# Six rows of a head per partition for q, k and v, with natural order restored on the way out of PSUM

## The chip, the core and the metric

One core of a Trainium2 chip runs the whole kernel. The metric is device time in microseconds (us), the median of several executions. The engines are PE (matrix products and transposes), ACT, DVE and POOL (elementwise work) and SP. SP issues the loads of q, k and v. POOL issues the loads of the weights, which are cast from fp32 to bf16 on the way, and can also compute.

## The reference

```python
# attention with a forget gate: B=8, H=8, S=576, D=64
scores = q @ k^T / sqrt(D);  cum = cumsum(log(clip(f)))
attn = softmax(where(causal, -1e9, scores + cum_i - cum_j))
x = (attn @ v) as (B, S, 512)
# spectral mixing: 64 complex modes, each with its own 512x512 weights (real and imaginary)
X = rfft(x, axis=1);  Y[:, :64] = X[:, :64] * (w_r + i w_i)   # per mode
u = x + irfft(Y);  out = u + relu(u @ w_ch)
```

The weights w_r and w_i are 134 MB of fp32; q, k and v are 28 MB together. Nothing is read twice.

## The kernel before

The attention has 32 steps. A step is one batch element `b` and one pair of heads, and `dc` numbers the pairs. Steps 0 to 7 are all batch elements of the first pair. The mode products of a pair need all eight batch elements, so they start after step 8 is under way. From then on each step also does two of the 64 weight groups. A ring of nine buffers prefetches weight groups.

```python
def emit_loads(s):                       # on SP, three stage tiles per tensor
    for d, src in zip(QKVst[s % STG], (q, k, v)):
        for h in range(2):
            nc.sync.dma_start(           # two rows of a head per partition: runs of 512 B
                d[:, h, 0:4, :].rearrange("p (a r) d -> p a (r d)", r=2),
                src[b, 2 * dc + h, 0:512, :].rearrange("(a p r) d -> p a (r d)", p=128, r=2))
        nc.sync.dma_start(d[0:64, :, 4, :], ...)   # the last 64 rows: runs of 256 B
...
for n in range(NRING):                   # on POOL, before anything else of substance
    emit_w_load(n)                       # two DMAs each, of 512 KB in bf16
nc.gpsimd.dma_start(wch[:], ...)
...
def emit_transposes(s):
    nc.scalar.copy(kb, stk_)             # ACT casts k
    nc.vector.tensor_copy(qb, stq_)      # DVE casts q
    nc.vector.tensor_tensor(va, stv_, decay, mult)   # DVE scales v: ready for attn @ v
    # k and q: five PE transposes each; contiguous evacuations, k on ACT, q on DVE
...
for s in range(NS + 1):
    emit_loads(s + 2); emit_transposes(s + 1)
    # scores, exp (ACT), causal masks (DVE), attn @ v, DFT of step s - 1
    if s > B:                            # modes: two weight groups a step
        for j in range(2):
            emit_modes(2 * (s - B - 1) + j)
            next_w()                     # POOL issues the next weight group
```

Because a partition holds rows 2p and 2p+1, the rows are in an interleaved order in this kernel, and its masks and its score blocks are arranged for that.

The softmax here doesn't subtract the row's maximum and nothing guards it: scores larger than these inputs give would overflow.

## Time and profile before

The median was 534.56 us (533.92 to 534.80, 3 runs). The profiled execution has a span of 533.4 us.

| stretch of the span, us | what happens | what limits it |
|---|---|---|
| 0 to 72 | weight prefetch, first steps | loads of q, k, v, about 12 us each |
| 72 to 118 | steps 3 to 9 | ACT, 5.66 us a step |
| 127 to 395 | steps and modes | loads again, DMA always full |
| 395 to 477 | rest of the weights | weight DMA |
| 477 to 533 | output | PE, ACT and DVE |

The first lines are from the page's table of 40 slices: the busy share in tenths for ACT and the DMA engines, and what the DMA moved in GB/s. Destination bytes are counted, so a weight byte of bf16 stands for two bytes read.

```profile
ACT  1033299997407152534264442554472332226564
...
DMA  9999985559999999999999999999999999982554
GB/s 160 212 212 213 211 199 153 146 148 209 212 212 212 211 212 212 211 211 212 212 212 213 212 211 213 212 212 211 209 207 207 206 207 207 207 136 90 218 226 178
```

The next view has the busy time of each engine in the stretches of the table above. Its last three columns are the granted PE clock, the DMA share, and GB/s. The share can exceed 1 because the records of packets overlap: with weights alone it is as high (1.21 from 395 to 477 us), since a weight packet is recorded at about 97 ns and one comes about every 80 ns on an engine.

```profile
core 0: us, PE busy (x) PEld busy (x) DVE busy (x) ACT busy (x) POOL busy (x), PEclk, DMA share, GB/s
0.00:72.00 72.00, 13.64 (x110) 9.29 (x112) 20.59 (x69) 19.44 (x24) 15.73 (x29) 0.91 1.16 203
72.00:118.00 46.00, 34.71 (x546) 25.75 (x553) 41.86 (x116) 45.52 (x66) 0.10 (x1) 1.00 0.57 155
127.00:395.00 268.00, 133.53 (x2552) 113.62 (x2570) 112.85 (x315) 116.02 (x158) 57.96 (x78) 0.69 1.21 211
395.00:477.00 82.00, 63.26 (x969) 41.83 (x979) 38.38 (x64) 23.62 (x40) 19.26 (x26) 0.95 1.21 202
477.00:533.00 56.00, 50.65 (x276) 23.87 (x279) 32.53 (x51) 30.22 (x53) 0.00 (x0) 0.96 0.45 171
```

In the second stretch ACT is busy 45.5 of 46 us while the DMA is half idle. In the third no engine is busy half the time, and the DMA is full. The chain of waits (start, duration, what) says which transfers matter:

```profile
11.51 12.14 DMA stq_115<-in_q_dram
...
48.50 11.97 DMA stv_114<-in_v_dram
...
87.66 1.56 ACT E_125 L385 x2
...
176.30 12.40 DMA stk_119<-in_k_dram
...
414.77 20.28 DMA wb<-in_moe_w_r_dram
```

The loads carry 28 MB against 134 MB of weights, yet they are the chain. The reason is in the queue table, here for 200 to 240 us (packets, MB, share of the 16 engines); q0 has the weights, q1 the loads:

```profile
q0 software_dynamic: 5916, 5.88, 86.4%
q1 hardware_dynamic: 5914, 2.54, 34.0%
```

The packets pair off one for one. A load packet has 512 or 256 B, and each one waits for a weight packet of 2048 B read. Last, two lines of POOL's timeline: the last initial issue, and the first issue after the modes have freed a ring buffer. I call the latter the first reissue; before it the ring is full.

```profile
45.11 0.74 POOL L214 DMA_DIRECT2D wch<-in_moe_w_ch_dram  x1 [2.74 <-DMA wb<-in_moe_w_r_dram]
117.90 0.74 POOL L80 DMA_DIRECT2D wb<-in_moe_w_r_dram  x1 [72.05 <-PE A L99]
```

### The profile page before, as it was taken

To read this page: it belongs to the slowest core of one execution; us is meant where nothing else is said; L and a number is where in the kernel's file an instruction comes from. 1 tells how busy PE (TensorE), PEld (TensorE's weight loads), DVE (VectorE), ACT (ScalarE), POOL (GpSimd) and SP (SyncE) were. 2 spreads that over 40 slices of the span, in tenths; PEclk is the share of its full clock that TensorE was granted. 3 is DMA by queue.
4 is the path that set the end of the run, shared out by engine and by line. 5 is a ranking of instruction groups with operands and counts; after the bars stand their busy time and mean duration, and the time that the engine had idled before them with its cause. 6 is when DMAs were issued, how large, how long until landed. Compare 5 with 4: busy or idle time off the path is not lost.

```text
span 533.4 us, 11332 instructions
## 1 busy us (share of the span) xinstructions
PE 304.2 (57%) x4637; PEld 221.4 (42%) x4684; DVE 254.6 (48%) x636; ACT 243.8 (46%) x352; POOL 97.4 (18%) x139
## 2 busy tenths in 40 slices
PE   0013077687516254645266353565488886669996
PEld 0002055465415243534155242454476544444442
DVE  4132079996415344443046243453584544435765
ACT  1033299997407152534264442554472332226564
POOL 6221000014211221221222122122232222100000
PEclk9999689999756767676567765677797999989999
DMA  9999985559999999999999999999999999982554
GB/s 160 212 212 213 211 199 153 146 148 209 212 212 212 211 212 212 211 211 212 212 212 213 212 211 213 212 212 211 209 207 207 206 207 207 207 136 90 218 226 178
DMA packets 137236, 106.28 MB, mean 199 GB/s; under 512 B 19360, under 2 KB 134560, under 8 KB 137184
## 3 DMA queue, kind: packets, MB, share of 16 engines
q0 software_dynamic: 68112, 67.64, 75.4%
q1 hardware_dynamic: 69072, 37.92, 30.7%
q8 instruction: 36, 0.59, 0.4%
q14 instruction: 16, 0.13, 0.1%
HBM read 163.73 MB, written 9.44 MB: 325 GB/s over the span
## 4 chain that ended last, share of the span: by engine, by line
DMA 75%; PE 12%; ACT 7%; DVE 2%; issue 2%; SPq 1%; ACTq 0%; DVEq 0%; POOLq 0%
DMA wb<-in_moe_w_r_dram 15%; DMA stv_114<-in_v_dram 9%; DMA stq_115<-in_q_dram 9%; DMA stk_119<-in_k_dram 9%; DMA stk_116<-in_k_dram 7%; DMA stq_112<-in_q_dram 7%; DMA stv_120<-in_v_dram 5%; DMA stq_118<-in_q_dram 5%; DMA stv_117<-in_v_dram 5%; DMA stk_113<-in_k_dram 4%; ACT E_126 L385 2%; ACT E_125 L385 2%; PE pz L569 2%; PE pu L561 2%; PE pz L565 2%
## 5 line engine op out<-in xcount | busy, mean ns | idle before, releaser
L80 POOL DMA_DIRECT2D wb<-in_moe_w_r_dram x64 | 47.7, 745 | 320.8 <-PE A L99 231.8
L99 PEld LDWEIGHTS <-wb 128*128 128x128 bf16 x2048 | 63.7, 99 | 33.6 <-DMA wb<-in_moe_w_i_dram 12.3
L385 ACT ACTIVATE E_125<-ps 128x1024 bf16<-128x1024 f32 x64 | 58.4, 966 | 13.5 <-PE ps L378 13.2
L385 ACT ACTIVATE E_126<-ps 128x1024 bf16<-128x1024 f32 x64 | 58.5, 960 | 7.6 <-PE ps L378 6.2
L80 POOL DMA_DIRECT2D wb<-in_moe_w_i_dram x64 | 48.0, 751 | 37.4 <-DMA wb<-in_moe_w_i_dram 37.3
L513 ACT CAST XW<-pxw 128x512 bf16<-128x512 f32 x40 | 23.1, 586 | 57.7 <-PE pxw L506 56.5
L350 PE MATMUL tp<-ident_bf,qb 128*128 128x128 bf16 x160 | 18.5, 257 | 52.9 <-ACT XT_1330 L445 21.5
L434 PE MATMUL px<-bas,x_all 128*128 128x128 bf16 x160 | 22.6, 244 | 37.8 <-DVE x_all L419 37.1
L506 PE MATMUL pxw<-wch,xT 128*128 128x512 bf16 x148 | 38.8, 387 | 1.3 <-DVE xT L502 0.6
L378 PE MATMUL ps<-QTs,KTz_0_123 128*128 128x64 bf16 (+5 forms) x128 | 29.1, 304 | 17.6 <-ACT E_126 L385 15.0
L378 PE MATMUL ps<-QTs,KTz_0_121 128*128 128x64 bf16 (+5 forms) x128 | 27.2, 287 | 20.4 <-ACT E_125 L385 17.4
L410 PE MATMUL pav<-va,E_125 128*128 128x65 bf16 x544 | 31.1, 216 | 13.4 <-DVE E_125 L397 11.0
L330 ACT CAST kb<-stk_116 128x640 bf16<-128x640 f32 x11 | 8.0, 728 | 66.5 <-DMA stk_116<-in_k_dram 66.5
L113 DVE TENSOR_TENSOR YT<-A,Yacc 128x256 bf16<-128x256 f32 x16 | 20.8, 1298 | 35.8 <-PE A L99 35.8
L357 DVE COPY QTs<-tp 128x576 bf16<-128x576 bf16 x32 | 14.6, 456 | 42.1 <-PE tp L350 41.3
L350 PEld LDWEIGHTS <-qb 128*128 128x128 bf16 x160 | 13.6, 113 | 49.2 <-issue 49.1
L350 PE MATMUL tp<-ident_bf,kb 128*128 128x128 bf16 x160 | 17.4, 248 | 28.6 <-ACT kb L330 16.5
L410 PEld LDWEIGHTS <-E_125 128*128 128x128 bf16 x544 | 27.0, 114 | 16.0 <-DVE E_125 L397 11.6
L576 DVE SCALAR_TENSOR_TENSOR uo<-pz,uo 128x512 f32<-128x512 f32 (+1 forms) x40 | 26.8, 688 | 12.6 <-ACT uo L575 12.4
L419 DVE TENSOR_TENSOR x_all<-pav,rcp 128x384 bf16<-128x384 f32 x64 | 31.1, 487 | 0.9
L397 DVE TENSOR_TENSOR E_125<-E_125,mask_74 128x512 bf16<-128x512 bf16 (+1 forms) x80 | 28.8, 380 | 5.4 <-ACT E_125 L385 4.6
L397 DVE TENSOR_TENSOR E_126<-E_126,mask_74 128x512 bf16<-128x512 bf16 (+1 forms) x80 | 28.7, 380 | 5.5 <-ACT E_126 L385 4.9
(121 smaller groups left out, 619.6 us busy)
## 6 DMA issues: line engine op xcount, KB each, us to landing
wb<-in_moe_w_r_dram POOLq DMA_DIRECT2D x64, 512.0 KB, 20.3
wb<-in_moe_w_i_dram POOLq DMA_DIRECT2D x64, 512.0 KB, 21.4
out_dram<-uo SPq DMA_DIRECT2D x16, 512.0 KB, 2.6
stq_112<-in_q_dram SPq DMA_DIRECT2D x22, 128.0 KB, 12.0
stk_113<-in_k_dram SPq DMA_DIRECT2D x22, 128.0 KB, 11.9
stv_114<-in_v_dram SPq DMA_DIRECT2D x22, 128.0 KB, 11.9
stq_115<-in_q_dram SPq DMA_DIRECT2D x22, 128.0 KB, 12.4
stk_116<-in_k_dram SPq DMA_DIRECT2D x22, 128.0 KB, 12.1
```

The source lines that it names most:

```text
L80: nc.gpsimd.dma_start(wb[:, t, :, :], src[g * MG : (g + 1) * MG, dc * 128 : (dc + 1) * 128, :].rearrange("m p e -> p m e"),)
L99: nc.tensor.matmul(A[:, eb, mi, :], lhsT=wb[:, t, mi, eb * 128 : (eb + 1) * 128], rhs=XT3[:, m, c0 : c0 + 2 * B], start=(t == 0), stop=(t ...
L350: nc.tensor.transpose(tp[:, sc * 128 : (sc + 1) * 128], src[:, sc, :, :].rearrange("p h d -> p (h d)"), ident_bf[:, :],)
L378: nc.tensor.matmul(ps[:, h, o : o + n], lhsT=KTz[s % NK][h][:, jb * 128 : (jb + 1) * 128], rhs=QT[s][:, CB[jb] + c0 : CB[jb] + c0 + n], st ...
L385: nc.scalar.activation(E[:, :, piece * 512 : piece * 512 + w], ps[:, :, 0:w], ACT.Exp, scale=scale,)
L397: nc.vector.tensor_tensor(dg, dg, tr, ALU.mult)
L410: nc.tensor.matmul(pav[:, i, h, :], lhsT=E[:, h, c : c + 128], rhs=va[:, jb, h, :], start=(jb == 0), stop=(jb == top),)
L419: nc.vector.tensor_tensor(x_all[:, b, sbs[0] : sbs[0] + n, dc * 128 : (dc + 1) * 128].rearrange("p c (h d) -> p c h d", h=2), pav[:, 0:n, ...
L434: nc.tensor.matmul(px[:, :, :], lhsT=x_all[:, b, sb, dc * 128 : (dc + 1) * 128], rhs=bas[:, sb, :, :], start=(sb == 0), stop=(sb == NSB - 1),)
L506: nc.tensor.matmul(pxw[:, :], lhsT=xT[:, eb, sb * 128 : (sb + 1) * 128], rhs=wch[:, eb, :], start=(eb == 0), stop=(eb == NDC - 1),)
L513: nc.scalar.copy(XW[:, b, sb, :], pxw[:, :])
L576: nc.vector.scalar_tensor_tensor(o_sb[:Ms, :], pz[:Ms, :], 0.0, u_sb[:Ms, :], ALU.max, ALU.add)
```

## The change

The intent is longer runs in HBM: with six rows of a head per partition (96 partitions) a run has 1536 B and a step's three tensors need three DMAs. The transposes then come out in the order (row within partition, partition). The PSUM evacuation reads them with a stride and so puts q and k in natural order, which lets the masks and the score blocks shrink. v needs rows on partitions, so it is transposed, put in order, and transposed back. For the first eight steps the cast of k and the scaling of v move to POOL.

```diff
     def emit_loads(s):
-        for h in range(2):
-            nc.sync.dma_start(d[:, h, 0:4, :]..., src[...]"(a p r) d -> p a (r d)", p=128, r=2)
-        nc.sync.dma_start(d[0:64, :, 4, :], src[..., 512:576, :]...)
+        nc.sync.dma_start(d[:, :, :, :]..., src[b, 2*dc : 2*dc+2]."h (p r) d -> p h (r d)", r=6)
...
     def emit_transposes(s):
+        early = s < B
-        nc.scalar.copy(kb..., stk_)
+        nc.gpsimd.tensor_copy(kv, stk_) if early else nc.scalar.copy(kv, stk_)
-        nc.vector.tensor_tensor(va[..., 0:Dh], stv_..., decay, ALU.mult)
+        (nc.gpsimd if early else nc.vector).tensor_tensor(vb, stv_..., decay6, ALU.mult)
-        for which, src in (("k", kb), ("q", qb)):      # 5 transposes of 128 rows
+        for which, src in (("k", kb), ("q", qb), ("v", vb)):   # 6 transposes of 96 rows
...
-            nc.vector.tensor_copy(QTs[:, :], tp[:, 0:S])
+            tv = tp.rearrange("c r p -> c p r")
+            nc.vector.tensor_copy(QTs.rearrange("c (p r) -> c p r", r=6), tv)   # k, v: same on ACT
+    def emit_vback(s):                   # after the last scores of step s
+        # five transposes of VT, then DVE copies to va
...
-    EOFF = [0, 576, 1152, 1472, 1792]; EW = 1920
+    EOFF = [0, 576, 1024, 1344, 1536]; EW = 1664
-    tr = mask3 (256 columns);  top = min(sb | 1, 4)
+    tr = trimask (128 columns); top = sb
...
-    out[...].rearrange("(p r) e -> p r e", r=2)       # 4-KB runs
+    out[...].rearrange("(r p) e -> p r e", r=2)       # 2-KB runs
```

## The prediction

> **What bounds it now.** The span of 533.4 us has four stages.
> (a) 0 to 72 us: the chain of waits is q/k/v loads of about 12 us each, since the weight prefetch runs beside them.
> (b) 72 to 118 us: the weight ring is full, and modes cannot start before step 8 is done. The ACT timeline repeats every 5.66 us a step, ACT 99% busy; DMA is half busy.
> (c) About 127 to 395 us: DMA always full (share 1.21, 212 GB/s by destination bytes); the chain is again loads of 12 to 13 us.
> (d) 395 to 477 us: weights alone, at 206 GB/s of destination, twice that of source; then a 56-us tail on PE, ACT and DVE.
>
> In one 40-us window of (c), the queue table has 5916 weight packets and 5914 load packets: the engines take one of each in turn. This agrees with the Trainium skill, "DMA: Bandwidth & Descriptors", section on queues, rings and completion order (engines alternate between queues by packet). From the packet records, source traffic is 359 GB/s in (c), 411 in (d). A weight packet costs an engine about 80 ns (estimate, 2048 B x 16 / 411 GB/s), so a load packet of 512 or 256 B takes about 32 ns of the rest. A step has 120 load packets an engine, which wait for 120 weight packets: 13.4 us, while its two weight groups need 129.
>
> **What the change does.**
> - Loads: 36 packets of 1536 B an engine and step. At my estimate of 60 to 65 ns each (extrapolated from 18 ns for 256 B and 27 ns for 512 B when alone), a step costs the DMA 2.3 us in place of 3.7. Loads stop being the chain; in (c) the weights become it, DMA still full. About 20 steps' loads come after the modes start: 28 to 30 us saved, all on the critical path.
> - Start: for the first eight steps the cast of k and the scaling of v move to POOL, behind the 19 initial weight issues, the last of which left at 45.1 us because eight DMAs may be outstanding. With loads quickly out of the way it should leave near 39 us. So step 0 starts LATER than before (scores near 46 us), but no loads hold the next steps.
> - Compute a step: ACT loses the k cast (0.74 us, early steps) and 256 of 1856 score columns a head (0.5), gains a v evacuation (0.7): 5.4 us early, 6.1 later. DVE loses mask columns (0.6), gains a strided, larger v-back copy. PE gains 13 transposes and loses four of 34 AV products: under ACT. POOL about 3 us a step. First modes at 46 + 7x5.4 + 2x6.1 + 4.6 = 101 us, against 118: 17 us saved. In (c) the extra compute has slack (6 us of PE in 12 us, at a granted clock of 0.67).
> - Tail: same bytes, 2-KB runs out for 4-KB ones; DMA is half idle there: nothing.
>
> **Sum.** 534.6 - 17 - 29 = about 488 us. Range 475 to 504. Faster by over 2%: 0.97, within 2%: 0.025, slower: 0.005.
>
> **What would show it.** First POOL cast near 40 us; first weight reissue near 101 us; load packets of 1536 B at 60 to 75 ns; chain in (c) on weight DMAs, not loads; source rate there near 395 GB/s; weights done near 430 us; tail still 56 us.
>
> **What would make it wrong.** POOL's cast and scaling over 5.5 us a step, or held back by DVE; strided PSUM reads costing ACT or DVE over 1.5 times; the two-buffer transpose pool, now five tiles a step, stalling PE; 1536-B packets costing as much per byte as the short ones.

## The result, and the profile after

The changed kernel takes 497.18 us (496.21 to 498.16, 4 runs) against 534.68 us before in the same rounds. The ratio is 0.9296, with a 95% interval of 0.9268 to 0.9324. Ratios here are the mean time of one kernel's fast runs over that of the other's fast runs of the same rounds, so not quite the ratio of the medians. The result is correct. Timed again later beside the last experiment, it took 495.70 us (ratio 0.9282).

The same lines of the page's 40 slices, after:

```profile
ACT  2202788999883444444444446662003122236564
...
DMA  9999998449999999999999999999999999923655
GB/s 205 264 206 211 267 273 228 143 148 236 260 255 233 234 234 234 234 234 234 234 235 232 234 219 207 207 206 208 205 207 207 206 206 207 207 48 136 230 207 192
```

The engines' busy times by stretch, after:

```profile
core 0: us, PE busy (x) PEld busy (x) DVE busy (x) ACT busy (x) POOL busy (x), PEclk, DMA share, GB/s
0.00:44.00 44.00, 4.18 (x18) 2.62 (x18) 12.31 (x43) 6.38 (x8) 15.16 (x28) 1.00 1.13 222
44.00:86.00 42.00, 30.66 (x405) 22.94 (x406) 34.58 (x73) 32.90 (x50) 18.51 (x17) 0.92 1.10 254
86.00:110.00 24.00, 18.60 (x315) 14.03 (x314) 20.97 (x57) 23.39 (x37) 0.31 (x1) 1.00 0.45 136
118.00:275.00 157.00, 102.81 (x1911) 84.71 (x1911) 84.81 (x226) 85.04 (x128) 35.95 (x48) 0.76 1.20 239
285.00:440.00 155.00, 108.63 (x1677) 74.52 (x1675) 67.09 (x144) 53.46 (x85) 38.75 (x53) 0.79 1.21 203
440.00:496.00 56.00, 51.14 (x280) 24.12 (x276) 32.25 (x51) 30.12 (x53) 0.00 (x0) 0.96 0.46 169
```

The mixed stage moves 239 GB/s in place of 211. The stretch of the tail is 56 us as before. For 44 us at the start PE and ACT do almost nothing, although loads of the first steps have landed. POOL's timeline has the reason:

```profile
43.50 0.74 POOL L214 DMA_DIRECT2D wch<-in_moe_w_ch_dram  x1 [1.80 <-DMA wb<-in_moe_w_r_dram]
44.24 0.83 POOL L347 CAST kb<-stk_114 96x768 bf16<-96x768 f32 x1
45.04 1.48 POOL L355 TENSOR_TENSOR vb<-stv_115,wdec_79 96x768 bf16<-96x768 f32 x1
...
49.45 1.47 POOL L355 TENSOR_TENSOR vb<-stv_121,wdec_79 96x768 bf16<-96x768 f32 x1
...
109.69 0.82 POOL L82 DMA_DIRECT2D wb<-in_moe_w_r_dram  x1 [32.23 <-PE A L101]
```

ACT's exp of a step's first scores shows when the step starts; I call it the first scores. Step 0 is at 49.70 us and step 7 at 93.95 us:

```profile
49.70 1.02 ACT L426 ACTIVATE E_128<-ps 128x1024 bf16<-128x1024 f32 x1
...
93.95 1.02 ACT L426 ACTIVATE E_129<-ps 128x1024 bf16<-128x1024 f32 x1
```

The first cast of k stands behind 19 weight issues in POOL's program. The trace never shows more than eight weight DMAs between issue and landing, so the later issues wait for earlier weights to land, and the cast waits with them. Still the first reissue comes at 109.7 us, 8.2 us earlier than before. The chain of waits after that is on weights, no longer on loads:

```profile
106.17 0.49 ACT E_129 L426
...
123.58 31.84 DMA wb<-in_moe_w_i_dram
...
232.50 25.59 DMA wb<-in_moe_w_i_dram
...
347.75 20.71 DMA wb<-in_moe_w_i_dram
```

The queue table for 190 to 230 us after the change has one load packet to three weight packets: the load queue is mostly empty.

```profile
q0 software_dynamic: 6488, 6.44, 96.4%
q1 hardware_dynamic: 2011, 2.87, 23.3%
```

**A balance.** I summed the trace's packet records in bins of 1 us, counting source bytes, from the first weight packet to the end of the last. With weights alone the rate is 411 GB/s. A bin under 300 GB/s is counted as a lull (its shortfall against 411 is time lost with the DMA waiting for work); the shortfall of all other bins is time lost with the DMA full.

| kernel | from first to last weight packet, us | lost in lulls | lost with the DMA full |
|---|---|---|---|
| before | 474.8 | 32.9 | 44.1 |
| changed | 435.7 | 24.4 | 14.6 |

The 39 us gained are 8.5 us of lulls and 29.5 us of better use; the 1 us between is in bins over 411 GB/s, which the table counts as no loss. The change leaves 24.4 us of lulls. The experiments ask two things: is packet size alone the cause of the better use, and is POOL's queue the cause of the lulls that remain?

### The profile page after: what moved, and what is told of

It reads as the page before. It is cut to its first block, busy times and chain, and to the rows that moved or that the text cites. A ratio compares the mean times of both kernels' runs of the same rounds, so it can differ in the third digit from the quotient of the medians.

```text
span 495.9 us, 11460 instructions
## 1 busy us (share of the span) xinstructions
PE 328.5 (66%) x4850; PEld 233.3 (47%) x4850; DVE 263.4 (53%) x624; ACT 243.1 (49%) x376; POOL 115.9 (23%) x154
## 4 chain that ended last, share of the span: by engine, by line
DMA 61%; PE 16%; ACT 7%; DVE 4%; issue 2%; POOL 0%; ACTq 0%; DVEq 0%; POOLq 0%
DMA wb<-in_moe_w_i_dram 61%; PE pxw L550 2%; PE pz L613 2%; PE pu L605 2%; PE pu L601 2%; PE pz L609 2%; ACT E_128 L426 2%; PE pyw L576 1%; PE ps L419 1%; ACT E_129 L426 1%; DVE qb L351 1%; PE tp L364 1%; DVE E_128 L441 1%; DVE XT_453 L485 1%; ACT KTz_1_127 L373 1%
## 5 line engine op out<-in xcount | busy, mean ns | idle before, releaser
L426 ACT ACTIVATE E_129<-ps 128x1024 bf16<-128x1024 f32 x64 | 53.5, 868 | 16.1 <-PE ps L419 15.8
L426 ACT ACTIVATE E_128<-ps 128x1024 bf16<-128x1024 f32 x64 | 53.2, 867 | 9.2 <-PE ps L419 9.1
L112 DVE TENSOR_TENSOR Yacc<-A,Yacc 128x256 f32<-128x256 f32 x32 | 14.1, 441 | 66.5 <-PE A L101 65.7
L101 PE MATMUL A<-XT_1366,wb 128*128 128x16 bf16 x512 | 20.1, 174 | 39.1 <-DMA wb<-in_moe_w_i_dram 36.8
L550 PE MATMUL pxw<-wch,xT 128*128 128x512 bf16 x160 | 43.8, 432 | 1.7 <-DVE xT L546 1.5
L101 PE MATMUL A<-XT_2871,wb 128*128 128x16 bf16 x512 | 19.7, 173 | 32.7 <-DMA wb<-in_moe_w_i_dram 28.7
L379 DVE COPY QTs<-tp 128x576 bf16<-128x576 bf16 x32 | 24.2, 756 | 32.2 <-PE tp L364 32.0
L373 ACT COPY KTz_0_124<-tp 64x576 bf16<-64x576 bf16 x16 | 10.3, 644 | 61.6 <-PE tp L364 61.6
L364 PE MATMUL tp<-ident_bf,kb 96*128 96x96 bf16 x192 | 19.2, 228 | 24.8 <-POOL kb L347 24.1
L373 ACT COPY KTz_0_126<-tp 64x576 bf16<-64x576 bf16 x16 | 10.5, 654 | 38.9 <-PE tp L364 38.8
L619 ACT COPY uo<-pu 128x512 f32<-128x512 f32 (+1 forms) x40 | 22.6, 586 | 11.6 <-PE pu L605 11.4
L419 PE MATMUL ps<-QTs,KTz_0_124 128*128 128x512 bf16 (+2 forms) x96 | 25.8, 324 | 3.6 <-ACT E_128 L426 2.0
L550 PEld LDWEIGHTS <-xT 128*128 128x128 bf16 x160 | 16.6, 110 | 24.1 <-issue 7.9
L419 PE MATMUL ps<-QTs,KTz_0_126 128*128 128x512 bf16 (+2 forms) x96 | 26.6, 332 | 1.9 <-ACT E_129 L426 0.9
L101 PE MATMUL A<-XT_4376,wb 128*128 128x16 bf16 x512 | 17.0, 171 | 16.4 <-DMA wb<-in_moe_w_i_dram 9.3
```

The costliest lines, as they stand in the source:

```text
L101: nc.tensor.matmul(A[:, eb, mi, :], lhsT=wb[:, t, mi, eb * 128 : (eb + 1) * 128], rhs=XT3[:, m, c0 : c0 + 2 * B], start=(t == 0), stop=(t ...
L364: nc.tensor.transpose(tp[:, r, :], src[:, r, :, :].rearrange("p h d -> p (h d)"), ident_bf[:RP, :RP],)
L373: nc.scalar.copy(KTz[s % NK][h][hs, 0:S].rearrange("c (p r) -> c p r", r=NR), tv[hs, :, :],)
L379: nc.vector.tensor_copy(QTs[:, :].rearrange("c (p r) -> c p r", r=NR), tv)
L419: nc.tensor.matmul(ps[:, h, o : o + n], lhsT=KTz[s % NK][h][:, jb * 128 : (jb + 1) * 128], rhs=QT[s][:, jb * 128 + c0 : jb * 128 + c0 + n] ...
L426: nc.scalar.activation(E[:, :, piece * 512 : piece * 512 + w], ps[:, :, 0:w], ACT.Exp, scale=scale,)
```

## The experiments

**1. The early casts off POOL.** One word of the changed kernel:

```diff
-            early = s < B
+            early = False
```

> The changed kernel with one word changed: the k cast and the v scaling of the first eight steps go to ACT and DVE, as in the later steps, and not to POOL. Theory A (in the changed kernel step 0 waits behind the blocked weight issues on POOL, until 44.2 us, and this delay reaches the end): step 0 starts near 22 us, steps of about 6.1 us as steps 7 to 9 of the changed kernel, first weight reissue near 82 us instead of 109.7, the DMA nearly never idle before the weights are done near 420 us, total 474 to 484 us. Rival B (the start is limited by the DMA or by ACT and DVE anyway, so POOL's wait costs little and its help is needed): 493 to 503 us.

Measured: 480.25 us, correct, ratio 0.8994 (0.8973 to 0.9016). Theory A held. POOL's timeline has no casts; the last initial issue comes later than in the changed kernel, since loads now take their turns, and the first reissue much earlier:

```profile
57.70 0.74 POOL L214 DMA_DIRECT2D wch<-in_moe_w_ch_dram  x1 [3.85 <-DMA wb<-in_moe_w_r_dram]
83.89 0.74 POOL L82 DMA_DIRECT2D wb<-in_moe_w_r_dram  x1 [25.44 <-PE A L101]
```

The DMA is full from 3 us on, so it is the one bound:

```profile
core 0: us, PE busy (x) PEld busy (x) DVE busy (x) ACT busy (x) POOL busy (x), PEclk, DMA share, GB/s
3.00:84.00 81.00, 52.63 (x729) 39.10 (x730) 62.56 (x167) 64.81 (x98) 13.48 (x19) 0.96 1.16 265
```

By the balance above, the weights take 417.1 us from first to last packet with 2.7 us of lulls. This is the best correct version. Its steps take about 5.8 us (casts of k on ACT at 43.62, 49.39 and 55.49 us). From step 1 to step 9 they take 5.7 us each, against 5.9 to 6.1 us in the two profiles of the changed kernel, so POOL's help made no step shorter.

**2. The casts on POOL, but ahead of the blocked issues.**

```diff
-        for n in range(NRING):
+        for n in range(4):
             emit_w_load(n)
-        nc.gpsimd.dma_start(wch[:], ...)
...
         emit_transposes(0)
+        emit_w_load(4)
         for s in range(NS + 1):
             ...
                 emit_transposes(s + 1)
+            if s < NRING - 5:
+                emit_w_load(5 + s)
+            elif s == NRING - 5:
+                nc.gpsimd.dma_start(wch[:], ...)
```

> The changed kernel with POOL still doing the early casts, but only eight weight DMAs are issued before the first cast; the other ten and wch are issued between the casts of the next steps. Theory A (it is the place in POOL's queue that costs): 474 to 486 us, like the run without POOL casts. Rival C (POOL as an engine is what costs: it holds up DVE, whose q cast took 4.4 us beside a run of POOL work against 0.55 us alone): clearly slower than the run without POOL casts, 487 us or more, with DVE ops stretched in each early step.

Measured: 483.24 us, correct, ratio 0.9040 (0.9013 to 0.9067). The place in the queue is most of the cost: with POOL still computing, 14 of the 17 us come back. The first reissue is at 93.4 us, later than in experiment 1, because casts and issues still alternate in one queue and a cast still waits behind an issue that waits for a weight: casts of k start at 25.44, 34.94 and 44.28 us, 9 us apart. So the total tells little about rival C, that POOL's work slows DVE. The traces do show it: beside POOL's work three masks on DVE took 1.5 to 2.6 us here and two casts of q 1.0 and 2.5 us, while in experiment 1 no recurring DVE instruction between 20 and 110 us ran 0.25 us over the median of its kind. What this adds to the total was not measured apart.

**3. The changed kernel with 512-B loads.**

```diff
-                nc.sync.dma_start(d[:, :, :, :]."p h r d -> p h (r d)", src[...]."h (p r) d -> p h (r d)", r=NR)
+                for h in range(2):
+                    nc.sync.dma_start(
+                        d[:, h, :, :].rearrange("p (a r) d -> p a (r d)", r=2),
+                        src[b, 2 * dc + h, :, :].rearrange("(a p r) d -> p a (r d)", p=RP, r=2))
```

> The changed kernel, but each partition's six rows are fetched as three runs of 512 B from three places in the head (so the result is wrong on purpose: rows are permuted): 108 load packets an engine and step in place of 36, all compute the same. Theory A (the gain of the mixed stage is packet size): 512-B packets cost about 32 ns of an engine beside weights, 3.5 us a step in place of 2.6; source rate in the mixed stage back from 396 to about 360 GB/s; first reissue a few us later; total 513 to 528 us. Rival D (the gain came from less compute: fewer score columns, smaller masks, fewer DMA instructions): 496 to 502 us.

Measured: 526.52 us (wrong result), ratio 0.9868 (0.9830 to 0.9906). Theory A held. The queue table for 200 to 240 us pairs off again:

```profile
q0 software_dynamic: 5788, 5.75, 84.5%
q1 hardware_dynamic: 5790, 2.81, 35.1%
```

The packet records give a source rate of 359 GB/s from 160 to 280 us, as before the change, against 396 with long packets. The first reissue falls back to 118.5 us. So all of the change but the packet size is worth about 8 us, and packet size in the changed kernel about 29 us. I did not follow up the 8 us; one part that the packet records show is that only 16.8 steps' loads are left at the first reissue, against 19.0 before. The cut also makes six DMAs of three in a step, and experiment 4 makes three of nine; the number of DMAs was not tested apart from the size of their packets.

**4. The kernel before with 1536-B loads.**

```diff
-            [stq.tile([128, 2, NSB, Dh], F32, ...) ...]
+            [stq.tile([128, 2, NSB + 1, Dh], F32, ...) ...]
...
-                # two DMAs with 512-B runs and one with 256-B runs
+                nc.sync.dma_start(
+                    d[0:96, :, :, :].rearrange("p h r d -> p h (r d)"),
+                    src[b, 2 * dc : 2 * dc + 2, :, :].rearrange("h (p r) d -> p h (r d)", r=6))
...
-                nc.vector.memset(t[64:128, :, 4, :], 0.0)
+                nc.vector.memset(t[96:128, :, :, :], 0.0)
...          # the compute reads stage rows 0:NSB, as many as before
```

> The kernel before, with only the loads changed: 96 partitions, runs of 1536 B into stage tiles of six rows, of which the compute reads five (wrong result on purpose, the same compute as before). Theory A: loads no longer hold the first steps, and nothing is on POOL, so steps run at 5.66 us each from about 22 us, first weight reissue near 78 us against 117.9, weights done near 420 us, total 473 to 484 us: more than the whole change brought. Rival E (packet size gives only the mixed stage's 28 us, the start needs the rest of the change): 500 to 508 us.

Measured: 477.64 us (wrong result), ratio 0.8939 (0.8922 to 0.8956). Theory A held in the total; the first reissue came at 82.7 us and not near 78. POOL's timeline:

```profile
59.47 0.74 POOL L209 DMA_DIRECT2D wch<-in_moe_w_ch_dram  x1 [3.90 <-DMA wb<-in_moe_w_r_dram]
...
82.71 0.74 POOL L80 DMA_DIRECT2D wb<-in_moe_w_r_dram  x1 [22.50 <-PE A L99]
```

The weights take 416.9 us from first to last packet, with 2.7 us of lulls: the same as in experiment 1. Long packets alone are worth 57 us when nothing stands in their way, and the changed kernel kept 37 us of it. The price of a correct result, natural order and v's detour included, is then only 480.25 against 477.64 us.

**5. Contiguous evacuation, twice.**

```diff
-                tv = tp[:, :, :].rearrange("c r p -> c p r")
+                tv = tp[:, :, :].rearrange("c r p -> c (r p)")
...          # and KTz, QTs, VTs written in that order, without (p r)
```

> The changed kernel, but the transposed q, k and v leave PSUM in the order in which they lie there, without the stride (wrong result on purpose: positions are permuted). DVE's q evacuation should fall from 0.76 us to the 0.46 us of before; ACT's evacuations should not change (0.63 us for 576 columns, against 0.69 for 640 before). Theory A (a step of the start is limited by ACT, 97% busy from 86 to 110 us): first reissue at most 2 us earlier, total 494 to 498 us. Rival F (strided evacuation is what made the steps 6.1 us and not 5.4): total 490 us or less.

Measured: 494.34 us (492.22 to 498.76; wrong result, not finite), ratio 0.9273 (0.9224 to 0.9323). That overlaps the changed kernel's, but the profiled execution was 490.5 us with its first reissue at 103.3 us, 6.4 us earlier and not at most 2. So I ran both together with more rounds.

> The changed kernel itself, to stand beside the run with contiguous evacuation on the same chip: 496 to 499 us.

> The same kernel as the run with contiguous evacuation, since its first timing spread from 492 to 499 us and its profile lay 5 us under the changed kernel's. Theory A (ACT limits the start): within 2 us of the changed kernel of this call. Theory F (the strided DVE evacuation limits part of the start): 4 us or more below it. In between: both count.

Measured: 495.70 us (494.96 to 498.24) for the changed kernel and 495.56 us (493.03 to 497.96) without the stride; ratios 0.9282 (0.9260 to 0.9305) and 0.9267 (0.9231 to 0.9303). The stride costs nothing that these rounds can show, though they can't exclude 1 or 2 us: in both profiles without it steps 7 to 9 took 4.6 us each (6.1 in both with it), and in the second pair the first reissue came at 105.9 against 108.4 us. The profile of the first try was a fast execution, and one profile is one execution. The price of the stride on DVE itself is real. The group of q evacuations before (busy us, mean ns):

```profile
L357 DVE COPY QTs<-tp 128x576 bf16<-128x576 bf16 x32 | 14.6, 456 | 42.1 <-PE tp L350 41.3 <-PE ps L378 0.5
```

After, with ACT's evacuation of v beside it:

```profile
L379 DVE COPY QTs<-tp 128x576 bf16<-128x576 bf16 x32 | 24.2, 756 | 32.2 <-PE tp L364 32.0
...
L384 ACT COPY VT_123<-tp 128x576 bf16<-128x576 bf16 x16 | 10.2, 636 | 3.5 <-PE tp L364 3.5
```

DVE takes 1.66 times as long for the same elements (756/456); without the stride it was 455 ns again. The Trainium skill, "VectorE: DVE Perf Modes", section on mode 2×_1P, says that two 16-bit elements a cycle need elements adjacent in memory; the ratio agrees with the loss of that mode, though no record here names the mode. ACT shows no such price: its evacuation of v took 636 ns with the stride and without it.

**6. Without v's detour.**

```diff
-            vb = qkb.tile([RP, NR, 2, Dh], ...); ...tensor_tensor(vb, stv_..., decay6, ALU.mult)
+            ...tensor_tensor(VAs[s % 3][0:RP, :, :, 0:Dh], stv_[:, :, 0:NSB, :]..., decay6, ALU.mult)
-            for which, src in (("k", kb), ("q", qb), ("v", vb)):
+            for which, src in (("k", kb), ("q", qb)):
...          # emit_vback keeps only the copy of the decay column
```

> The changed kernel, but v is scaled straight from its stage tile into the tile of the product, five of six rows, and not transposed twice (wrong result on purpose). It takes 11 transposes, one ACT evacuation (0.63 us) and one DVE copy (0.48 us) from each step, the loads and the place of the casts stay. Theory A: steps of the start fall from about 6.1 to 5.5 us, first reissue near 104 us against 109.7, total 489 to 493 us: the detour costs some 5 us, only in the start. Rival G (the detour has slack everywhere): 495 to 498 us.

Measured: 486.36 us (wrong result, not finite), ratio 0.9104 (0.9069 to 0.9139). The detour costs about 10 us of the changed kernel, twice what theory A gave it, so the time lies below theory A's range. The first reissue is at 101.7 us. The first scores of steps 0 and 9 are at 51.13 and 96.98 us, so a step takes 5.1 us; in the changed kernel they are at 49.70 and 106.17 us, 6.3 us a step. So the detour costs 1.2 us a step and not the 0.6 us of its ACT evacuation. The three parts (transposes, two more tiles through the two transpose buffers, ACT and DVE copies) were removed together and are not told apart.

**7. Both: casts off POOL and no detour.** The diff is that of 1 and 6 together.

> The same removal of the v detour (wrong result on purpose), made in the kernel whose early casts are off POOL (480.25 us). Theory A (there the DMA is full from 3 us until the last weight lands, so compute has slack everywhere before the tail): 477 to 481 us, within 1%. Rival H (steps of the start still count there): 475 us or less.

Measured: 476.06 us (475.09 to 476.35; wrong result), ratio 0.8901 (0.8880 to 0.8921): between the two expectations. The weights take 416.5 us from first to last packet against 417.1 in experiment 1, so shorter steps bring no faster DMA, as theory A said. The 4.2 us lie nearly all after that stretch. After the last weight has landed, the first output product starts 7.5 us later in experiment 1 (420.96 to 428.44) and 3.4 us later here (420.64 to 423.99). In between PE runs 20 channel products (`pxw`, 6.25 us at a granted clock of 0.77 over the gap) in experiment 1 and 10 (2.32 us at 1.00) here; why PE has more of them left at the end with the detour was not settled. So the detour also costs after the loads: the 2.6 us between experiments 1 and 4 lie there as well (57.1 against 53.8 us from the last landing to the end).

| kernel | us | first reissue at, us | first to last weight packet, us | lulls, us |
|---|---|---|---|---|
| before | 534.68 | 117.9 | 474.8 | 32.9 |
| changed | 497.18 | 109.7 | 435.7 | 24.4 |
| 1: casts off POOL | 480.25 | 83.9 | 417.1 | 2.7 |
| 2: casts before the issues | 483.24 | 93.4 | 421.5 | 7.4 |
| 3: changed, 512-B loads | 526.52 | 118.5 | 462.9 | 28.4 |
| 4: before, 1536-B loads | 477.64 | 82.7 | 416.9 | 2.7 |
| 6: no v detour | 486.36 | 101.7 | 429.8 | 18.2 |
| 7: 1 and 6 | 476.06 | 81.0 | 416.5 | 2.2 |

## Why the prediction was right or wrong

The direction and the bounds held: 488 us predicted, 497.18 measured, inside 475 to 504. Of the 46 us foreseen 37.5 came. By the two profiles, the start gave 8.2 us (first reissue) in place of 17, the stretch from there to the last weight 31.0 in place of 29, and what follows took 1.7 us more. The miss is in the start.

- *"The engines take one of each in turn"*: right. The pairing vanishes with long packets (6488 to 2011) and returns when only the packet size is put back (experiment 3). The Trainium skill's "DMA: Bandwidth & Descriptors", section on queues, rings and completion order, describes such a turn by packet; its packet may hold several descriptors, and the equal counts here show equal shares, not how many records go in one turn.
- *"28 to 30 us saved" in the mixed stage*: right in sum, and by luck so near. From the first reissue to the landing of the last weight it was 361.0 us before (117.9 to 478.9) and 329.9 us after (109.7 to 439.6), so 31.0 us. Terms in it were off and nearly cancelled. A load packet of 1536 B costs an engine about 73 ns beside weights and not 60 to 65 (estimate: at 325 GB/s of weights an engine spends 0.79 us of each us on them at 80 ns, and shares the rest among 2.85 load packets), so a step costs 2.6 to 2.7 us, not 2.3. A record of such a packet alone, from 86 to 108 us, has 65 ns: I had taken the cost alone for the cost in the mix. By the same working, with 294 GB/s of weights and 8.6 load packets, a step had cost 4.0 us before, not 3.7. And 16.9 steps' loads were left at the first reissue, by packet count, in place of 19.0 before; I had put about 20 on both sides.
- *"In (c) the weights become the chain", "source rate near 395 GB/s", "tail still 56 us"*: right. The rate was 396 GB/s and the tail 56 us by the stretches above; from the landing of the last weight to the end it was 54.5 us before and 56.2 after, with 4.6 and 6.8 us of it before the first output product.
- *"Step 0 starts LATER than before"*: half right. Its cast of k did wait behind the issues (44.24 us, against 14.34 before), and experiment 1 shows that this costs 17 us. I took it as given and counted only the gain beside it. But its first scores reached ACT at 49.70 us, earlier than before (53.54 us): there DVE had stood in its program at a load of v that landed at 46.7 us. The last initial issue left at 43.5 us, not 39, and the first scores came at 49.7 us, not 46: load packets were dearer, and 2112 of them, 3.7 steps' worth and not 3, ran in the first 31 us.
- *"5.4 us early, 6.1 later"*: this is the step that failed. The later steps took 6.1 us, as said. The early ones took 6.3 us (first scores of step 0 at 49.70 and of step 7 at 93.95 us), which is 6.4 us over seven steps. I had added up ACT's work alone and taken ACT for the limit. From 49.70 to 93.95 us ACT was busy 84% and DVE 87%, and experiment 1 gave the cast of k back to ACT without a longer step. Experiment 6 shows one part: v's detour costs 1.2 us a step at the start, while I had charged it 0.7 us on ACT and called PE and DVE "under ACT". POOL's work beside DVE, shown below, is another part, not sized. The first step took 7.9 us and the other six 6.06 each.
- *"First modes at 101 us"* (100.6 before rounding): 109.7. The sum of the parts is 3.7 (first scores) + 6.4 (early steps) − 1.1 (from the last scores to the reissue, 3.5 us and not 4.6) = 9.0 us.
- *What would make it wrong*: POOL needed 2.3 us a step (0.83 + 1.48), so its rate was no limit; its place in the program was. The strided evacuation did cost DVE 1.66 times, over the 1.5 I had named, and in experiment 5 this was under what the rounds resolve.
- A wait that I had named only as a risk did show. While POOL ran six casts and scalings without a gap, one cast of q on DVE took eight times its usual time, and beside later POOL work six masks took 0.84 to 1.35 us, the one below four times its usual time:

```profile
46.98 4.36 DVE L351 CAST qb<-stq_119 96x768 bf16<-96x768 f32 x1
...
51.93 0.54 DVE L351 CAST qb<-stq_113 96x768 bf16<-96x768 f32 x1
...
64.56 1.15 DVE L441 TENSOR_TENSOR E_128<-E_128,trimask 128x256 bf16<-128x256 bf16 x1
...
66.20 0.26 DVE L441 TENSOR_TENSOR E_128<-E_128,trimask 128x256 bf16<-128x256 bf16 x1
```

The cast ended at 51.3 us, just after POOL's first gap at 50.9 us. The Trainium skill, "SBUF — State Buffer", section "SBUF: two separate sides", says that POOL and DVE, the latter in some modes or with two inputs in SBUF, share a port pair by an exclusive lock. The times agree with that. That POOL's work causes the waits is shown: the six masks lost 4.7 us in all, and in the four kernels without it (before, experiments 1, 4 and 7) no cast of q took over 0.8 us. That the lock is the means is argued. The wait of the cast alone does not set the step: in experiment 6 the same cast took 3.71 us and the first step 4.9 us.

## What to carry to other kernels

When two DMA queues compete and one has short packets, count packets and not bytes: here the short queue moved one small packet for each large one of the other (5914 to 5916), and it became the chain although it carried few bytes. Compute that was put on POOL ran only after the DMA issues ahead of it, the first cast at 44.24 us; look at an engine's program order before giving it work that the first step needs, and at what its work does to its neighbours. When a transfer-bound kernel is improved, measure its lulls: after this change they were 24 us, and one word removed 17 us of the total.

## What the Trainium skill lacked or had wrong

- "DMA: Bandwidth & Descriptors", Specifications, gives 512 B as the minimum transfer for line rate. Beside a second queue 512-B packets left 359 GB/s of source traffic, 1536-B packets 396, weights alone 411. No page gives the cost of such a mix. Estimates from these rates: 35 ns an engine for 512 B (experiment 3) and 73 ns for 1536 B, so about 16 ns that do not depend on size, if a weight packet costs 80 ns beside loads too.
- The same page's section "Why small descriptors are slow" puts the fixed part inside a DMA engine at about 3 cycles a packet, 3.5 ns at the 850 MHz of the page's Specifications (estimate); the 16 ns estimated here for a packet in the mix are much more than that.
- The Specifications of the same page give about 358 GB/s as the HBM limit of a core, half of what two cores share. With one core running, the traces show 411 GB/s of reads, near the 408.7 that the page's own table has for one stream alone. So this is no error of the page, but its first table taken alone misleads for a single core.
- "SBUF — State Buffer" says that the loser of the shared port pair blocks for the winner's instruction. A cast of q on DVE took 4.36 us in place of 0.54, through four POOL instructions in a row, not one.
- No page warns that a DMA issue on POOL which waits until earlier transfers land holds the compute behind it. Here that held step 0 until 44.2 us and cost 17 us (497.18 against 480.25 us).
